# Seven-product first layers from block 11, exponentials read from PSUM, and a last tile stored in three pieces

## The chip, the cores and the metric

The kernel runs on one core of one Trainium2 chip. The metric is device time in microseconds (us), the median of the runs shown. An execution is one launch that goes through attention, one feed-forward layer and one gated layer for 36 tiles of 128 tokens.

## The reference

What is computed, cut to its steps (B = 8, 8 heads, 576 tokens, heads of 64, model width 512):

```python
# 1. attention in chunks of 64 tokens
scores = q_c @ k_c.T / 8
attn = exp(scores - scores.max(-1)); attn /= attn.sum(-1) + 1e-9
x = attn @ v_c                                  # [B, 576, 512]
# 2. a feed-forward layer
xn = (x - mean(x)) / sqrt(var(x) + 1e-6) * g_ln
x = x + relu(xn @ w_ch1) @ w_ch2                # 512 -> 2048 -> 512
# 3. a gated layer
u, v = split(gelu(x @ w_in))                    # 512 -> 2 * 512
v_s = w_sg @ (norm(v) * g_ln2) + b_sg           # over the 576 tokens
out = x + (u * v_s) @ w_out
```

## The kernel before

Every number goes through the matrix engine as a pair of 16-bit halves, so that a product of two tiles takes three matmuls (high by high, high by low, low by high).

Work is cut into **units** of 128 tokens (t = 0 to 35, attention and norm) and **blocks** of two units (b = 0 to 17, the feed-forward layer); the gated layer follows for all of them in a second part. Blocks 0 to 2 multiply in the plain way. From block B0 = 3 the second layer (`ff2p`, line 1005) takes **seven products** where eight would be plain. The first layer has two forms. `ff1p` (line 854, blocks 3 to 11) is plain: 192 matmuls of 256 columns in a block, in eight steps j of 24. `ff1s` (line 923, from block BS = 12) takes seven products over the block's two units: 336 matmuls of 128 columns. For `ff1s` the first-layer weights are summed and split again beforehand: `sums_w1` makes the sums, `move_w1` puts a part of them in place during the last `ff1p` block, and `norm7` (for units from 2*BS) prepares the block's input.

The weights of the gated layer are prepared during blocks 3 to 8 (`prep`, `halve`, `pieces`): ACT scales a piece into a scratch tile (`Btmp`), ACT copies the high half, DVE subtracts it for the low half. There is one scratch tile, so a piece's scaling waits for the subtraction of the one before. `sums_w1` starts when all pieces are done and stored (`close_st`).

A unit from t = 10 on goes like this. SP loads q and k (`qkl`) and v. PE makes the scores in one half of a PSUM pair (`qk`, line 302). DVE takes the maximum (line 400) and subtracts it into `pml` (line 401), ACT takes the exponential in place (line 404). ACT and DVE split that into two halves, SP turns them by DMA (line 415), and PE multiplies with v (`pv_`, line 360). The matmuls of lines 302 and 360 work on 64 by 64 parts of the array, all others of this stretch on the whole 128 by 128. The scores of unit t+1 are part of the same entry as `pv_` of unit t:

```python
o("PE", 1260, lambda: (pv_(), qk_()), rd=pp() + [a_], wr=[kp, ks])
```

The order on each engine is set by a **planner** (class `Plan`): each entry has an engine, a cost in ns, what it reads and writes, a latency and a priority; the planner simulates the engines and emits, on each, the entry of the lowest priority number among those that are ready. Attention has the numbers 10*t, the matmuls of the two layers have 1000 and up in the order of writing, what follows them on ACT and DVE has about -100, and the weights' preparation 8000 to 9000, so that it fills gaps. On the chip each engine takes its instructions in that order and waits for what they need.

The last tile of the second part (`o_unit`, line 2050) is done in two halves of 256 columns: for each half a slot of the ring `xp` is loaded (line 2044), DVE adds (line 2055), SP stores (line 2058).

Of the kernel before, what the change touches and what calls it, by code (L numbers as in the profile page):

```python
# [51 lines left out]
BS = 12  # L52
# [96 lines left out]
def fused_kernel(ctx: ExitStack, tc, qkv, w1, w2, g1, w_in, w_out, wsgt, wsgs, g2, b_sg, out):  # L149
# [162 lines left out]
    def attention(t):  # L312
# [19 lines left out]
        pm = palloc("pm", 2, [P, 4, 2, 64], F32) if t < JOIN else palloc("pml", 1, [P, 4, 2, 64], F32)  # L332
# [58 lines left out]
        def sums():  # L391
# [9 lines left out]
        o("DVE", 600, lambda: nc.vector.tensor_tensor(  # L401
            out=pm.t.rearrange("p h a k -> p a h k"), in0=sv, in1=mx.t.to_broadcast([P, 2, 4, 64]), op=ALU.subtract
        ), rd=[ks, mx], wr=[pm])
        o("ACT", 520, lambda: nc.scalar.activation(out=pm.t, in_=pm.t, func=AF.Exp, scale=0.125), wr=[pm], **far)
# [62 lines left out]
    def norm7(t, x, o):  # L467
# [38 lines left out]
        xT = xT_t[b] = plan.buf("xTD", 2, lambda: dl["all"][:, 7680 + n * 3584:11264 + n * 3584].rearrange(  # L506
# [578 lines left out]
    def open_b():  # L1085
        close_pool("sums")
        bW["wBp"] = tc.tile_pool(name="wB", bufs=1)
        wB = bW["wBp"].__enter__()
        bW["win"] = late[:, 0:8192].rearrange("p (k x e) -> p k x e", k=4, x=2)
        bW["winT"] = late[:, 8192:16384].rearrange("p (k u x n e) -> p k u x n e", k=2, u=2, x=2, n=4)  # L1090
        for nm, sh in (("wout", [P, 4, 2, D]), ("wsg", [P, 5, 2, S])):
            bW[nm] = wB.tile(sh, F16, name=nm)
        bW["stp"] = tc.tile_pool(name="stB", bufs=1)
        bW["st"] = bW["stp"].__enter__()
        bW["top"].t = bW["st"].tile([P, 1024], F32, name="top")
        nc.vector.memset(bW["top"].t, 0.0)
# [7 lines left out]
    half = []  # L1104

    def prep(nm, srcs):
# [37 lines left out]
    def halve(nm, n, i, m, q, full, ck):  # L1144
# [3 lines left out]
        def fin():  # L1148
# [11 lines left out]
        tmp = plan.buf("Btmp", 1, lambda: bW["st"].tile([P, 1024], F32, tag="tmp", name="tmp", bufs=1))  # L1160
# [3 lines left out]
            out=tmp.t[:, 0:P], in_=row.partition_broadcast(P)[:, 0, :]  # L1164
        ), rd=[f"redd{i}"], wr=[tmp], prio=pr, lat=5000)
        op("DVE", 220, lambda: nc.vector.tensor_reduce(
            out=col(nm + "_e"), in_=tmp.t[:, 0:P], axis=AX.X, op=ALU.max
# [53 lines left out]
    def sums_w1(j):  # L1221

        pr = 8000 + j
        n = j % 2
# [135 lines left out]
    with tc.manual_schedule():  # L1360
# [79 lines left out]
        half.append(prep("wsg", [wv[k] for k in range(4)] + [wsgs]))  # L1440
        done = [f"winT{k}{uv}" for k in range(2) for uv in range(2)] + [f"win{k}" for k in range(4)] + [f"wout{k}" for k in range(2)] + [f"wsg{k}" for k in range(5)]
        op(None, 0, lambda: None, wr=[f"w1_{j}" for j in range(8)], prio=0)
        todo = []
        for b in range(B0, BS):
# [10 lines left out]
            if b == B0 + 4:  # L1455
                op(None, 0, close_st, rd=["wsg_s"] + done + [f"{k}D" for k in done], wr=["Braw", "Btmp", "topB", "w1s"] + done, prio=0)
                for j in range(8):
                    sums_w1(j)
                op(None, 0, lambda: None, wr=["wb0", "wb1", "wt0", "wt1", "xTD0", "xTD1", "xTD0l", "xTD1l"], prio=0)
# [572 lines left out]
        def o_unit(g, i, more=False):  # L2032
# [5 lines left out]
            parts = 2 if t == NG * GT - GT + 4 else 1  # L2038
            for q in range(parts):
                (key, ap), = take(1)  # L2040
                m = 512 // parts
                fc = slice(q * m, q * m + m)
                xr = o_ring(more)
                do("SP", 730, lambda xr=xr, fc=fc: nc.sync.dma_start(out=xr.t[:, fc], in_=x2d[t][:, fc]), [], [xr], lat=2200)
# [8 lines left out]
                for h in range(2):  # L2053
                    pe(1300 // parts, lambda h=h, mm=mm: mm(h), ["gt0", "gt1"] if i == 4 else [f"gp{i // 5}{2 * h + k}" for k in range(2)], [key])
                do("DVE", 730 // parts, lambda xr=xr, fc=fc, ap=ap, m=m: nc.vector.scalar_tensor_tensor(
                    out=xr.t[:, fc], in0=ap[:, 0:m], scalar=col(cn), in1=xr.t[:, fc], op0=ALU.mult, op1=ALU.add
                ), [key, cn], [xr], 1000)
                do("SP", 730, lambda xr=xr, fc=fc: nc.sync.dma_start(out=out[t][:, fc], in_=xr.t[:, fc]), [xr], [], lat=2200)
# [142 lines left out]
```

## Time and profile before

| | |
|---|---|
| runs | 1161.77, 1162.14, 1162.97 us, median 1162.14 |
| the profiled execution | 1161.08 us, its span 1159.3 us |
| PE (matmuls), busy | 1143.9 us, 99% of the span |
| PEld (weight loads), busy | 896.1 us, 77% |
| DVE, busy | 956.7 us, 83% |
| ACT, busy | 729.4 us, 63% |
| POOL, busy | 171.2 us, 15% |
| TensorE clock granted, mean | 0.992 |
| chain that ended last, by engine | PE 92%, DVE 3%, DMA 2% |

Busy time and share of the span are for one engine each, and engines work beside each other. The chain is followed back from the last instruction, at each step to what released it. A matmul's own duration (273 ns for 256 columns) is longer than the distance to the next, since matmuls overlap; what counts for the time is that distance, from start to start.

### The profile page before, as it was taken

Reading aid. Unit: us, or ns where it says so; the run is one execution under the profiler, and the core shown is the slowest. Engines: PE = TensorE matmul, PEld = TensorE weight load, DVE = VectorE, ACT = ScalarE, POOL = GpSimd, SP = SyncE. Lnnn points to the kernel's source line nnn. Section 1 sums busy time; section 2 is a strip of 40 time slices with the busy share of each in tenths; the row PEclk is TensorE's granted clock in tenths of the full one; section 3 lists DMA queues with packets and bytes.
Section 4 is the critical chain, followed back from the end, with each engine's and each line's share of the span. In section 5 each row is a group of like instructions: output and inputs, shape, how many; then the busy total and the mean of one; then the engine's idle time right before and its main releaser. Section 6 shows DMA issues by size and latency. Waiting matters only on the chain.

```text
span 1159.3 us, 30389 instructions
## 1 busy us (share of the span) xinstructions
PE 1143.9 (99%) x12866; PEld 896.1 (77%) x12866; DVE 956.7 (83%) x1757; ACT 729.4 (63%) x1231; POOL 171.2 (15%) x285
## 2 busy tenths in 40 slices
PE   7999999999999999999999999999999999999998
PEld 5788448888888888888999999998566558558554
DVE  6997796999888899999887887896888688788555
ACT  5787645668667776666566666565748647646621
POOL 2211010223313223201011001001202101101100
PEclk7999999999999999999999999999999999999999
DMA  8964016546444532414352431696355481392203
GB/s 286 285 237 133 19 29 219 170 129 140 124 122 122 155 93 65 102 47 92 102 88 57 107 70 34 156 272 180 74 112 162 91 181 56 109 178 78 91 1 109
DMA packets 182824, 141.36 MB, mean 122 GB/s; under 512 B 142624, under 2 KB 151712, under 8 KB 182688
## 3 DMA queue, kind: packets, MB, share of 16 engines
q1 hardware_dynamic: 182688, 139.43, 45.3%
q8 instruction: 100, 1.64, 0.6%
q14 instruction: 36, 0.29, 0.1%
HBM read 79.46 MB, written 25.59 MB: 91 GB/s over the span
## 4 chain that ended last, share of the span: by engine, by line
PE 92%; DVE 3%; DMA 2%; ACT 1%; issue 1%; SPq 0%; POOL 0%; DVEq 0%; ACTq 0%
PE acc L1005 23%; PE bank L854 16%; PE bank L923 9%; PE pb L1853 4%; PE acc L1853 4%; PE pair L759 4%; PE bank L738 4%; PE acc L1741 3%; PE pb L1741 3%; PE pb L1799 3%; PE acc L1799 3%; PE pb L2050 3%; PE acc L1989 2%; PE bank L759 2%; PE pair L302 2%; PE pb L1989 1%
## 5 line engine op out<-in xcount | busy, mean ns | idle before, releaser
L1005 PEld LDWEIGHTS <-arena 128*128 128x128 f16 x2016 | 194.0, 98 | 22.3
L854 PE MATMUL bank<-xTo,w1all 128*128 128x256 f16 x1728 | 201.1, 273 | 0.0
L854 PEld LDWEIGHTS <-w1all 128*128 128x128 f16 x1728 | 168.5, 98 | 20.1
L1005 PE MATMUL acc<-w,arena 128*128 128x256 f16 x1152 | 174.2, 273 | 0.0
L1005 PE MATMUL acc<-w2s,arena 128*128 128x256 f16 x864 | 142.2, 273 | 0.0
L881 ACT ACTIVATE arena<-arena 128x896 f16<-128x896 f32 x72 | 68.2, 947 | 40.5 <-PE acc L1005 24.9
L882 DVE TENSOR_TENSOR arena<-arena 128x896 f16<-128x896 f32 x72 | 80.6, 1120 | 8.1 <-ACT arena L881 7.4
L869 ACT ACTIVATE arena<-bank 128x512 f32<-128x512 f32 x72 | 42.5, 591 | 51.8 <-PE bank L854 48.5
L923 PE MATMUL bank<-dL,w1all 128*128 128x128 f16 x1152 | 73.3, 219 | 1.1 <-ACT arena L936 0.5
L1741 PEld LDWEIGHTS <-x2T 128*128 128x128 f16 x672 | 65.5, 98 | 9.9
L923 PEld LDWEIGHTS <-w1all 128*128 128x128 f16 x1152 | 68.3, 98 | 2.6 <-issue 1.5
L1799 PEld LDWEIGHTS <-w1all 128*128 128x128 f16 x336 | 32.9, 98 | 38.4 <-issue 0.7
L738 PEld LDWEIGHTS <-w1all 128*128 128x128 f16 x576 | 54.8, 98 | 9.4 <-issue 1.6
L923 PE MATMUL bank<-dL,late 128*128 128x128 f16 x864 | 60.0, 219 | 0.3
L923 PEld LDWEIGHTS <-late 128*128 128x128 f16 x864 | 53.4, 98 | 2.0 <-issue 0.6
L1853 PEld LDWEIGHTS <-vh 128*128 128x128 f16 x288 | 28.5, 99 | 33.5
L1005 PEld LDWEIGHTS <-dL 128*128 128x128 f16 x504 | 47.1, 98 | 5.2 <-DVE dL L979 0.5
L1871 ACT ACTIVATE w2s<-uT 128x512 bf16<-128x512 f32 x30 | 18.8, 627 | 49.2 <-DVE uT L1867 43.8
L1853 PE MATMUL pb<-late,vh 128*128 128x512 f16 x150 | 46.7, 380 | 0.0
L738 PE MATMUL bank<-xTo,w1all 128*128 128x256 f16 x384 | 44.9, 273 | 0.9 <-DMA xTo<-hl 0.7
L1005 PE MATMUL acc<-w,dL 128*128 128x256 f16 x288 | 44.2, 273 | 0.2 <-DVE dL L979 0.2
L1853 PE MATMUL acc<-late,vh 128*128 128x512 f16 x138 | 42.6, 380 | 0.0
(390 smaller groups left out, 2672.6 us busy)
## 6 DMA issues: line engine op xcount, KB each, us to landing
straw<-in_w SPq DMA_DIRECT2D x16, 1023.8 KB, 6.3
qkl<-in_qkv SPq DMA_DIRECT2D x26, 512.0 KB, 3.8
x2d<-x SPq DMA_DIRECT2D x36, 256.0 KB, 2.0
vl<-in_qkv SPq DMA_DIRECT2D x26, 256.0 KB, 3.2
xz<-x2d SPq DMA_DIRECT2D x22, 256.0 KB, 3.4
xs<-x2d SPq DMA_DIRECT2D x21, 256.0 KB, 3.2
qk<-in_qkv SPq DMA_DIRECT2D x10, 512.0 KB, 5.1
wD<-late SPq DMA_DIRECT2D x8, 512.0 KB, 2.9
```

The source lines that it names most:

```text
L738: nc.tensor.matmul(acc, lhsT=w[j][:, k, fc], rhs=xT.t[:, x, k], start=(n == 0), stop=(n == 11))
L759: nc.tensor.matmul(acc[i], lhsT=h[x].t[:, c], rhs=w2t[j][:, f % 2, y], start=(f == 0 and n == 0), stop=(f == NF - 1 and n == 2),)
L854: nc.tensor.matmul(acc[:, y * 256:y * 256 + 256], lhsT=w[j][:, k, fc], rhs=xT.t[:, x, k], start=(n == 0), stop=(n == 11),)
L869: op("ACT", 500, lambda: nc.scalar.activation(out=o.t[:, 0:4].rearrange("p n t -> p (n t)"), in_=acc, func=AF.Relu, scale=0.5), rd=[kb] + ...
L881: op("ACT", 860, lambda: nc.scalar.activation(out=h.t[:, 0], in_=o.t[:, 1:8], func=AF.Copy), rd=[o] + ar, wr=[h], prio=-100)
L882: op("DVE", 1010, lambda: nc.vector.tensor_tensor(out=h.t[:, 1], in0=o.t[:, 1:8], in1=h.t[:, 0], op=ALU.subtract), rd=[o, h], wr=[h.key + ...
L923: nc.tensor.matmul(ap, lhsT=left(p, j, w, k), rhs=xT.t[:, x, SEVEN[p] * 2 + k], start=(first and n == 0), stop=(k == 1 and w == 1), skip_g ...
L1005: nc.tensor.matmul(acc, lhsT=h.at(x, n), rhs=r(y), start=(first and j == 0 and m == 0), stop=(j == 7 and m == 2), skip_group_check=True,)
L1741: nc.tensor.matmul(ap[:, q * 256:q * 256 + 256], lhsT=xT[:, x, a, k, c], rhs=right(b, 1, k, w), start=(first and n == 0), stop=(k == 1 and ...
L1799: nc.tensor.matmul(ap, lhsT=right(b, 0, k, w)[:, m * 128:m * 128 + 128], rhs=xT[:, x, a, k], start=(first and n == 0), stop=(k == 1 and w ...
L1853: nc.tensor.matmul(ap, lhsT=v[:, fc], rhs=w[:, 0:512], start=(n == 0), stop=end)
L1989: nc.tensor.matmul(bk[1][:, q * 256:q * 256 + 256], lhsT=gs[e][x][h][:, c:c + 128], rhs=r, start=(first and n == 0), stop=(k == 1 and x == ...
```

## The change

- **Seven-product first layers in seven blocks.** BS goes from 12 to 11: block 11 takes `ff1s` in place of `ff1p`, units 22 and 23 take `norm7`, `move_w1` runs during block 10. The scratch places of `sums_w1` and of the `xTD` buffers are laid out anew for it.
- **Weights' splits through three buffers.** `Btmp` becomes three scratch tiles (`rt`, cut in three, two of which are also the place of the raw load).
- **Exponentials per head from PSUM.** In units 10 to 21 the subtraction on DVE and the exponential over 512 columns go. POOL makes the maximum times -0.125, and ACT takes eight exponentials of 64 columns from PSUM with it as bias. `pml` gets two buffers.
- **`pv_` and `qk_` are two entries of the planner**, for all units from 10 on.
- **Last tile in pieces** of 256, 128 and 128 columns, with one load for all.

```diff
-BS = 12
+BS = 11
@@ attention
-        pm = ... palloc("pml", 1, [P, 4, 2, 64], F32)
+        pm = ... palloc("pml", 2, [P, 4, 2, 64], F32)
...
+        if 10 <= t < 22:
+            def less():
+                nc.gpsimd.tensor_scalar(out=mx.t, in0=mx.t, scalar1=-0.125, scalar2=0.0, op0=ALU.mult, op1=ALU.add)
+            def exps(a, hs):
+                for h in hs:
+                    nc.scalar.activation(
+                        out=pm.t[:, h, a], in_=s2[:, a, h * 64:h * 64 + 64], func=AF.Exp, scale=0.125, bias=mx.t[:, a, h]
+                    )
+            o("POOL", 300, less, wr=[mx], two=2)
+            for a_, hs in [(a_, range(h_, h_ + 4 // 4)) for a_ in range(2) for h_ in range(0, 4, 4 // 4)]:
+                o("ACT", 190, lambda a_=a_, hs=hs: exps(a_, hs), rd=[ks, mx], wr=[pm], **far)
+        else:
+...
...
-            o("PE", 1260, lambda: (pv_(), qk_()), rd=pp() + [a_], wr=[kp, ks])
+            o("PE", 330, pv_, rd=pp(), wr=[kp])
+            o("PE", 450, qk_, rd=[a_], wr=[ks])
@@ prep, halve, pieces
+    def rtmp(k):
+        c = (2048, 0, 1024)[k]
+        return plan.buf(f"Btmp{'abc'[k]}", 1, lambda: bW["rt"][:, c:c + 1024])
...
-            tmp = plan.buf("Btmp", 1, lambda: bW["st"].tile([P, 1024], F32, tag="tmp", name="tmp", bufs=1))
+            nt3[0] += 1
+            tmp = rtmp(nt3[0] % 3)
@@ sums_w1
-        n = j % 2
+        n = j % 2 if j < 6 else (NB - BS) % 2
@@ o_unit
-            parts = 2 if t == NG * GT - GT + 4 else 1
-            for q in range(parts):
+            xr = o_ring(more)
+            do("SP", 730, lambda: nc.sync.dma_start(out=xr.t, in_=x2d[t]), [], [xr], lat=2200)
+            for c, m in ((0, 256), (256, 128), (384, 128)) if t == NG * GT - GT + 4 else ((0, 512),):
                 (key, ap), = take(1)
-                m = 512 // parts
-                fc = slice(q * m, q * m + m)
-                xr = o_ring(more)
-                do("SP", 730, lambda xr=xr, fc=fc: nc.sync.dma_start(out=xr.t[:, fc], in_=x2d[t][:, fc]), [], [xr], lat=2200)
+                fc = slice(c, c + m)
```

The planner is run anew, so every engine's order moves from block 3 on. Three places:

**PE, the end of unit 20 in the kernel before** (`ptt` and `vq` are the two operands of `pv_`, `qkl` holds q and k of the next unit, `pair` is the PSUM pair; line 1005 is the second layer):

```order
L360 LDWEIGHTS ptt
L360 MATMUL pair_67<-vq,ptt 64x64
L302 MATMUL pair_67<-qkl 64x64 x16
L1005 LDWEIGHTS arena
L1005 MATMUL acc_2383<-w2s,arena 128x256
L1005 LDWEIGHTS arena
L1005 MATMUL acc_2383<-w2s,arena 128x256
```

**PE, the scores of the same next unit in the changed kernel** (line 870 is `ff1p`, 1021 the second layer):

```order
L870 LDWEIGHTS w1all
L870 MATMUL bank_69<-xTo,w1all 128x256
L302 MATMUL pair_67<-qkl 64x64 x16
L1021 LDWEIGHTS arena
L1021 MATMUL acc_2383<-w_5_176,arena 128x256
L1021 LDWEIGHTS arena
L1021 MATMUL acc_2383<-w_5_176,arena 128x256
```

**PE, a `pv_` in the changed kernel**, the next one behind those scores:

```order
L360 LDWEIGHTS ptt
L360 MATMUL pair_67<-vq,ptt 64x64
L360 LDWEIGHTS ptt
L360 MATMUL pair_67<-vq,ptt 64x64
L1021 LDWEIGHTS arena
L1021 MATMUL acc_2384<-w_1_172,arena 128x256
L1021 LDWEIGHTS arena
```

Before, 25 of the 26 score groups stand right behind a `pv_`; now one does, and the other 25 stand between whole-array matmuls, as one did before.

**ACT in block 5, from the first-layer result of its third step on**, before (line 869 is that result's ReLU, 881 its high half, 1199 and 1202 a weight piece's scaling and high half, 779 a maximum):

```order
L869 ACTIVATE arena<-bank_68 128x512
L1202 ACTIVATE late<-tmp 128x1024
L779 ACTIVATE u,x2mx<-x 128x512
L869 ACTIVATE arena<-bank_69 128x512
L881 ACTIVATE arena<-arena 128x896
L1199 ACTIVATE tmp<-late,c_win_s 128x1024
L1202 ACTIVATE late<-tmp 128x1024
L881 ACTIVATE arena<-arena 128x896
```

and changed, from the same ReLU (now lines 885 and 897; 1146 is a maximum of a weight, 408 an exponential of one head):

```order
L885 ACTIVATE arena<-bank_68 128x512
L408 ACTIVATE pml<-pair_67,mx 128x64
L1146 ACTIVATE rt,mxc<-wsg 128x576
L408 ACTIVATE pml<-pair_67,mx 128x64
L1146 ACTIVATE rt,mxc<-wsg 128x576
L408 ACTIVATE pml<-pair_67,mx 128x64
L1146 ACTIVATE rt,mxc<-wsg 128x576
L408 ACTIVATE pml<-pair_67,mx 128x64
L1146 ACTIVATE rt,mxc<-wsg 128x576
L408 ACTIVATE pml<-pair_67,mx 128x64
L795 ACTIVATE u,x2mx<-x 128x512
L897 ACTIVATE arena<-arena 128x896
L885 ACTIVATE arena<-bank_69 128x512
```

Exponentials of 64 columns now stand between the other work, and two scalings in a row become possible further on.

**SP, the last rows**, before (2044 loads a slot, 2058 stores):

```order
L2044 DMA xr_12738<-x2d_110 128x512
L2058 DMA out<-xr_12739 128x512
L2044 DMA xr_12739<-x2d_106 128x256
L2058 DMA out<-w2s 128x512 x3
L2058 DMA out<-g_12742 128x512
L2058 DMA out<-xr_12738 128x512
L2044 DMA w2s<-x2d_106 128x256
L2058 DMA out<-xr_12739 128x256
L2058 DMA out<-w2s 128x256
```

and changed (2065 loads, 2083 stores):

```order
L2065 DMA xr_12937<-x2d_110 128x512
L2083 DMA out<-xr_12938 128x512
L2065 DMA xr_12938<-x2d_106 128x512
L2083 DMA out<-w2s 128x512 x3
L2083 DMA out<-g_12941 128x512
L2083 DMA out<-xr_12937 128x512
L2083 DMA out<-xr_12938 128x256
L2083 DMA out<-xr_12938 128x128 x2
```

The second load of the last tile is gone from between the last stores, and the first loads all 512 columns.

## Rows read from the trace of the kernel before

**Rows 1.** The page's part 1: busy us, share, instructions of each engine

```profile
PE 1143.9 (99%) x12866; PEld 896.1 (77%) x12866; DVE 956.7 (83%) x1757; ACT 729.4 (63%) x1231; POOL 171.2 (15%) x285
```

**Rows 2.** Timeline of PE in block 11: start us, busy us, line, what, count

```profile
508.06 2.78 PE L854 MATMUL bank<-xTo,w1all 128*128 128x256 f16 x24
510.68 0.49 PE L1005 MATMUL acc<-w,arena 128*128 128x256 f16 x3
```

**Rows 3.** Timeline of PE in block 12, seven-product first layer

```profile
551.96 0.83 PE L923 MATMUL bank<-dL,late 128*128 128x128 f16 x12
552.63 0.49 PE L1005 MATMUL acc<-w2s,arena 128*128 128x256 f16 x3
```

**Rows 4.** Timeline of PE where pv_ and the next scores follow each other

```profile
411.52 0.49 PE L1005 MATMUL acc<-w2s,arena 128*128 128x256 f16 x3
411.94 0.58 PE L360 MATMUL pair<-vq,ptt 64*64 64x64 f16 x48
412.35 0.70 PE L302 MATMUL pair<-qkl 64*64 64x64 f32 x32
412.97 0.83 PE L1005 MATMUL acc<-w,arena 128*128 128x256 f16 x6
```

**Rows 5.** Timeline of PE where scores stand alone

```profile
187.42 0.82 PE L1005 MATMUL acc<-w,arena 128*128 128x256 f16 x6
188.16 0.69 PE L302 MATMUL pair<-qkl 64*64 64x64 f32 x32
188.79 0.50 PE L1005 MATMUL acc<-w2s,arena 128*128 128x256 f16 x3
```

**Rows 6.** Timeline of PE where a pv_ stands alone

```profile
704.04 0.83 PE L923 MATMUL bank<-dL,late 128*128 128x128 f16 x12
704.81 0.58 PE L360 MATMUL pair<-vq,ptt 64*64 64x64 f16 x48
705.32 0.50 PE L1005 MATMUL acc<-w,dL 128*128 128x256 f16 x3
```

**Rows 7.** Timeline of all engines at the end

```profile
1152.07 2.78 PE L2050 MATMUL pb<-late,w2s 128*128 128x256 f16 x24
...
1153.58 0.48 DVE L2055 SCALAR_TENSOR_TENSOR xr<-pb,c_c_m,xr 128x256 f32<-128x256 f32 x1 [0.56 <-PE pb L2050]
...
1155.97 0.48 DVE L2055 SCALAR_TENSOR_TENSOR w2s<-pb,c_c_m,w2s 128x256 f32<-128x256 f32 x1 [1.90 <-DMA w2s<-x2d]
1156.48 0.33 SPq L2058 DMA_DIRECT2D out<-w2s  x1
```

**Rows 8.** Whom PE waited for, 177 to 800 us: total, times, longest

```profile
PE bank L923 <- ACT arena L936: 0.5, 1, 0.5
PE bank L923 <- DVE dL L939: 0.4, 1, 0.4
PE bank L923 <- DVE arena L939: 0.3, 1, 0.3
PE acc L1005 <- DVE dL L979: 0.2, 1, 0.2
```

**Rows 9.** DVE from block 4 to block 7: window, its length, busy

```profile
239.60:344.50 104.90, 91.89 (x185) 1.00 0.53 130
```

**Rows 10.** ACT in the same window

```profile
239.60:344.50 104.90, 73.10 (x111) 1.00 0.53 130
```

**Rows 11.** Groups of DVE by shape: count, busy us, mean ns, idle before

```profile
L401 DVE TENSOR_TENSOR pml<-pair,mx 128x512 f32<-128x512 f32 x26 | 17.6, 678 | 0.0
...
L1205 DVE TENSOR_TENSOR late<-tmp,late 128x1024 f16<-128x1024 f32 x8 | 9.7, 1214 | 0.6 <-ACT late L1202 0.6
```

**Rows 12.** Groups of ACT by shape

```profile
L936 ACT ACTIVATE dL<-bank 128x256 f32<-128x256 f32 x48 | 18.3, 381 | 37.5 <-PE bank L923 33.8 <-DVE dL L979 2.6 <-DVE x L1030 0.9
...
L404 ACT ACTIVATE pml<-pml 128x512 f32<-128x512 f32 x26 | 16.1, 620 | 1.6 <-DVE pml L401 1.5
...
L1035 ACT ACTIVATE u<-acc,c_c2a 128x256 f32<-128x256 f32 x13 | 6.1, 472 | 1.1 <-PE acc L1005 0.7
```

More of the change, by code (lines that the diff above doesn't have):

```diff
@@ L331, in attention @@
         mx = palloc("mx", 2, [P, 2, 4, 1], F32)
-        pm = palloc("pm", 2, [P, 4, 2, 64], F32) if t < JOIN else palloc("pml", 1, [P, 4, 2, 64], F32)
+        pm = palloc("pm", 2, [P, 4, 2, 64], F32) if t < JOIN else palloc("pml", 2, [P, 4, 2, 64], F32)
         sm = palloc("sm", 2, [P, 4, 2, 1], F32)
@@ L400, in attention @@
         o("DVE", 600, lambda: nc.vector.tensor_reduce(out=mx.t, in_=sv, axis=AX.X, op=ALU.max), rd=[ks], wr=[mx])
[L401 to L404, printed above, removed]
+        if 10 <= t < 22:
[10 more added lines that the diff above has]
+        else:
+            o("DVE", 600, lambda: nc.vector.tensor_tensor(
+                out=pm.t.rearrange("p h a k -> p a h k"), in0=sv, in1=mx.t.to_broadcast([P, 2, 4, 64]), op=ALU.subtract
+            ), rd=[ks, mx], wr=[pm])
+            o("ACT", 520, lambda: nc.scalar.activation(out=pm.t, in_=pm.t, func=AF.Exp, scale=0.125), wr=[pm], **far)
         if t < BYDMA:
@@ L505, in norm7 @@
         plan.count["xTD"] = n - 1 if n else 1
-        xT = xT_t[b] = plan.buf("xTD", 2, lambda: dl["all"][:, 7680 + n * 3584:11264 + n * 3584].rearrange(
+        xT = xT_t[b] = plan.buf("xTD", 2, lambda: dl["all"][:, 7680 + n * 4096:11264 + n * 4096].rearrange(
             "p (x n t) -> p x n t", x=2, t=128
@@ L1095, in open_b @@
         bW["top"].t = bW["st"].tile([P, 1024], F32, name="top")
+        bW["rt"] = bW["st"].tile([P, 3072], F32, name="rt")
         nc.vector.memset(bW["top"].t, 0.0)
@@ L1163, in halve @@
         op("SP", 100, lambda: nc.sync.dma_start(
-            out=tmp.t[:, 0:P], in_=row.partition_broadcast(P)[:, 0, :]
+            out=bW["top"].t[:, 0:P], in_=row.partition_broadcast(P)[:, 0, :]
         ), rd=[f"redd{i}"], wr=[tmp], prio=pr, lat=5000)
         op("DVE", 220, lambda: nc.vector.tensor_reduce(
-            out=col(nm + "_e"), in_=tmp.t[:, 0:P], axis=AX.X, op=ALU.max
+            out=col(nm + "_e"), in_=bW["top"].t[:, 0:P], axis=AX.X, op=ALU.max
         ), rd=[tmp], wr=[nm + "_r"], prio=pr)
@@ L1455, in fused_kernel @@
             if b == B0 + 4:
-                op(None, 0, close_st, rd=["wsg_s"] + done + [f"{k}D" for k in done], wr=["Braw", "Btmp", "topB", "w1s"] + done, prio=0)
+                op(None, 0, close_st, rd=["wsg_s"] + done + [f"{k}D" for k in done], wr=["Btmpa", "Btmpb", "Btmpc", "topB", "w1s"] + done, prio=0)
                 for j in range(8):
                     sums_w1(j)
-                op(None, 0, lambda: None, wr=["wb0", "wb1", "wt0", "wt1", "xTD0", "xTD1", "xTD0l", "xTD1l"], prio=0)
+                for n in range(2):
+                    op(None, 0, lambda: None, wr=[f"wb{n}", f"wt{n}", f"xTD{n}", f"xTD{n}l"], prio=0)
             block(b + 2)
@@ L2053, in o_unit @@
                 for h in range(2):
-                    pe(1300 // parts, lambda h=h, mm=mm: mm(h), ["gt0", "gt1"] if i == 4 else [f"gp{i // 5}{2 * h + k}" for k in range(2)], [key])
-                do("DVE", 730 // parts, lambda xr=xr, fc=fc, ap=ap, m=m: nc.vector.scalar_tensor_tensor(
+                    pe(1300 * m // 512, lambda h=h, mm=mm: mm(h), ["gt0", "gt1"] if i == 4 else [f"gp{i // 5}{2 * h + k}" for k in range(2)], [key])
+                do("DVE", 130 + 600 * m // 512, lambda fc=fc, ap=ap, m=m: nc.vector.scalar_tensor_tensor(
                     out=xr.t[:, fc], in0=ap[:, 0:m], scalar=col(cn), in1=xr.t[:, fc], op0=ALU.mult, op1=ALU.add
-                ), [key, cn], [xr], 1000)
-                do("SP", 730, lambda xr=xr, fc=fc: nc.sync.dma_start(out=out[t][:, fc], in_=xr.t[:, fc]), [xr], [], lat=2200)
+                ), [key, cn, xr][:2 + (m < 512)], [xk], 1000)
+                do("SP", 730, lambda fc=fc: nc.sync.dma_start(out=out[t][:, fc], in_=xr.t[:, fc]), [xk], [], lat=2200)
         def wout_sums():
```

9 lines of the change are left out of this document (6 added, 3 removed).

## Prediction

> **What bounds the kernel now.** I read the page's first part, then the waits of PE, then PE's timeline at the places the change touches. PE is busy for 99% of the span, every other engine less [rows 1], and the chain of the table above is PE for 92% of it. The waits of PE from 177 to 800 us are four short ones, 1.4 us together, all in the blocks with seven-product first layers; none is in blocks 3 to 11 [rows 8]. So from block 3 on the time is the sum of the distances between matmul starts. An edit counts by what it adds to or takes from that sum, and by any new wait of PE. Only at the very end does something else come last: DVE's last addition starts when a load has landed, not when PE is done [rows 7].
>
> **Block 11 in seven products.** Plain: 24 matmuls of 256 columns take from 508.06 to 510.68, that is 0.109 us each [rows 2]; the block's 192 take 20.9 us. Seven products: 12 matmuls of 128 columns take from 551.96 to 552.63, 0.056 us each [rows 3]; 336 take 18.8 us. **Minus 2.2 us**, all of it on PE. The second layer stays as it is, and the first block of the new form with its start-up only moves one block earlier.
>
> The trace shows 0.056 us between 128-column matmuls although each has its own weight load [rows 3]. [...] The row decides: twelve in a row here take 0.67 us.
>
> **The last tile.** Before, PE's run of 24 matmuls ends at 1152.07 + 2.78 = 1154.85, but the last addition starts at 1155.97, held by the second load, takes 0.48 and the store is issued at 1156.48 [rows 7]. Now one load, early, feeds all pieces, and the order has no load between the last stores. PE's run keeps its length (12 x 0.109 + 24 x 0.056 = 2.65 against 24 x 0.109 = 2.62). The first half's addition begins at 1153.58, right when its twelve matmuls are through, so I let the last one follow PE at once: 1154.9, plus an addition of 128 columns (between 0.24, half of the 0.48 for 256, and 0.48; I take 0.36) gives 1155.3 for the store, against 1156.48. **Minus 1.2 us**; minus 0.9 if three stores close together land later, minus 1.5 if half the bytes land sooner.
>
> **`pv_` and `qk_` as two entries.** The words for the change don't mention it, and it is the largest term. No matmul is added. But these two work on 64 by 64 parts of the array, their neighbours on the whole, and each change between the two costs PE time. Together: the whole-array group before them would end at 411.52 + 3 x 0.109 = 411.85, the next whole-array matmul starts at 412.97: the pair takes 1.12 us of PE [rows 4]. Scores alone: 187.42 + 6 x 0.109 = 188.07 to 188.79, 0.72 us [rows 5]. A `pv_` alone: 704.04 + 0.67 = 704.71 to 705.32, 0.61 us [rows 6]. Apart they cost 0.72 + 0.61 - 1.12 = 0.21 us more. By the order, scores stand alone 25 times where they stood alone once: 24 x 0.2 = **plus 4.9 us** (4.8 to 5.0). Nothing hides it: PE has no waits there that it could fill [rows 8].
>
> [...]
>
> **Exponentials from PSUM.** In 12 units DVE loses a subtraction of 0.68 us [rows 11] and ACT an exponential of 0.62; ACT gets eight of 64 columns [rows 12]. No row shows one. An ACT pass from PSUM over 256 columns takes 0.38 us, with a scale per partition 0.47 [rows 12]; from 512 columns (0.62) to 256 (0.38) a column costs 0.93 ns, so 64 columns with a bias per partition come to 0.47 - 192 x 0.00093 = 0.29 us (0.12 if all of the 0.47 went by columns, 0.47 if none did). Eight take 2.4 us, 1.8 more than before. ACT is not the bound, so by itself this costs nothing. It counts where PE waits for it: the scores of the next unit now stand in PE's queue right behind these exponentials, whose PSUM they overwrite, and all of PE's matmuls are queued behind them. The planner reckons 8 x 0.19 = 1.5 us for the eight and keeps 1.0 us until the scores; the eight take 0.9 longer. So this cover is almost used up: between 0 and 0.4 us in each of 12 units.
>
> **Splits through three buffers.** The same work, earlier. Between the middle of block 4 and block 7 DVE is busy for 91.9 of 104.9 us [rows 9] and ACT for 73.1 [rows 10], so 13.0 and 31.8 are free. Counting the instructions between the same first-layer steps in both orders, each at its group's mean, DVE gets 14.3 us more there (the largest item four more weight pieces of 1.22, against five subtractions of 0.68 [rows 11]) and ACT some 30 with exponentials at 0.29. Both engines are full there. What covers it: a first-layer result is needed only two steps later, and no row of blocks 3 to 11 has PE wait for one [rows 8]. The summed weights for the first new block are done in DVE's order before step 6 of block 10, so block 11 doesn't wait for them.
>
> For the new waits of both kinds I take **plus 0.6 us**: from minus 0.8 (some of the 1.4 us of present waits fall away with the new order) to plus 5 (12 times 0.4).
>
> **Sum.** -2.2 - 1.2 + 4.9 + 0.6 = +2.1 us. The profiled execution, 1161.08 us, would be 1163.2; it lies 1.1 under the median, so the median 1162.14 becomes **1164.2**. A measurement of this kernel can tell about 0.2%, 2.3 us: faster is under 1159.8, slower over 1164.5.
>
> **The rivals.**
> - *PE waits for the exponentials and for two full engines.* Place: the scores behind the exponentials, units 10 to 21, and the second layer in blocks 4 to 7. It decides from an exponential of 0.31 us on, where eight are a full microsecond over the planner's figure. At 0.35 the eight take 2.8, 0.3 past the cover, 12 times: 3.6 us in place of 0.6, **1167.2**, slower. For it: both windows are full [rows 9, 10]. Against: PE itself runs later than the planner thinks by the very cost of the separate entries, which gives the others time. 17 in 100.
> - *The separate entries cost nothing*, since other waits would have stood in the same place: -2.2 - 1.2 + 0.6 = -2.8, **1159.3**, faster. Against it are three places that agree [rows 4 to 6] and a queue without waits. 5 in 100.
> - [...] 4 in 100.
> - *128-column matmuls go at the pace of their weight loads.* PEld is busy 896.1 us for 12866 loads [rows 1], 0.070 each: 336 would take 23.4, plus 2.5 where I have minus 2.2, **1168.9**, slower. [...] Against it stands the 0.67 for twelve [rows 3]. 1 in 100.
> - *The seven-product part doesn't pay*, since the new block brings waits like those of the six present ones, 1.4 us for six [rows 8], 0.2 each: too small to be told apart, in the 0.6.
>
> **How the numbers follow.** The forecast has 73 in 100; with 1161.8 to 1166 as its own spread around 1164.2, close under the line of 1164.5, I give 47 of them to within 0.2% and 26 to slower. With the rivals: faster 5, within 0.2% 51, slower 44. Leaving out the upper part of the first rival, the second and the fourth, the range is 1161.8 to 1167.0.
>
> **What would show it.** Right: the lone scores of the changed kernel take 0.72 us from whole-array matmul to whole-array matmul, the lone `pv_` 0.61; block 11 is some 2 us shorter apart from that; the last addition follows PE; PE's waits from 177 to 800 us stay under 3 us. Wrong: scores that wait for ACT in the waits of PE (first rival), or a pair apart that costs no more than 1.12 (second).

## The result, and the profile after

The changed kernel is slower: 1173.88 us median (1171.22 to 1174.9) against 1162.56, a ratio of 1.0103 with a 95% interval of 1.0087 to 1.0119. The prediction was 1164.2, with a range up to 1167.0. The sign of its sum was right, and three of its four terms; the fourth, the new waits, was far too small.

The profiled execution took 1171.22 us, its span 1169.4 (before: 1159.3). It lies 2.7 under the median of its kernel; what the three others spend more isn't known, since they have no trace. So the accounts below explain a rise of 10.1 us, that of the profiled executions, and not quite the 11.3 of the medians. The page's part 1 of the changed kernel, for [rows 1]:

```profile
PE 1146.0 (98%) x13022; PEld 894.5 (76%) x13022; DVE 955.3 (82%) x1746; ACT 744.1 (64%) x1326; POOL 172.3 (15%) x295
```

PE is busy hardly longer (2.1 us), while the span grew by 10.1: most of the rise is time in which PE stood idle. Whom PE waited for in the changed kernel, 177 to 805 us (total, times, longest), for [rows 8]:

```profile
PE pair L302 <- ACT pml L408: 4.2, 1, 4.2
PE pair L360 <- DMA ptt<-ph: 2.0, 1, 2.0
PE bank L939 <- ACT arena L952: 0.9, 2, 0.5
PE pair L360 <- DVE mx L400: 0.9, 1, 0.9
```

Two waits of block 5 are new and long: scores on an exponential (L408), `pv_` on the turned `ptt`. The chain of waits of the changed kernel in that stretch (start, us, what) tells where the first comes from:

```profile
270.31 7.62 DMA redd<-redc
...
278.05 0.33 SPq L1186
...
278.48 4.53 DMA x2d<-x
...
283.13 0.70 DVE x L457
...
283.85 0.32 ACT pml L408
...
284.22 1.13 PE pair L302 x32
285.35 2.67 PE bank L870 x12
```

Read it from the top. `redd<-redc` stores the 128 maxima of one weight, 4 bytes from each partition; line 1186 loads them back, all 128 to every partition. That load stands on SP's queue right behind the store, and SP stands at it until the store has landed, 7.6 us later. The stores of `x` to `x2d` are queued behind. DVE's write of a unit's attention into `x` (L457) needs the buffer that one of them empties and waits 7.8 us for it, the last of the eight exponentials of a unit waits 5.8 us for L457, and PE's next scores wait for that exponential. The wait of DVE, and what SP stood at its loads in all (the second time for 8.8 us, until 303.2; the `ptt` that PE waits for 2.0 us could be turned only behind that, at 303.70):

```profile
DVE x L457 <- DMA x2d<-x: 7.8, 1, 7.8
```

```profile
SPq L1186 <- DMA redd<-redc: 15.8, 2, 8.8
```

Then the clock: windows ahead of the long wait, behind it, and later (start and end, length, busy us with the number of instructions for PE, PEld, DVE, ACT and POOL, granted clock, DMA share, GB/s):

```profile
256.96:279.70 22.74, 22.74 (x321) 19.85 (x319) 16.79 (x37) 19.34 (x47) 9.72 (x12) 1.00 0.42 115
284.22:290.00 5.78, 5.78 (x55) 4.31 (x56) 5.71 (x13) 5.49 (x7) 1.64 (x4) 0.50 0.78 147
290.20:300.00 9.80, 9.80 (x135) 8.61 (x134) 9.73 (x18) 9.17 (x16) 5.74 (x6) 1.00 0.33 124
```

After PE had stood still for 4.2 us its granted clock was 0.50 for 5.8 us, and 1.00 again in the window from 290.20: by the account below that cost 2.3 us.

The order had shown the cause, in rows that I did not read. SP in block 5 in the kernel before:

```
L1162 DMA redd_73<-redc 128x1
L1163 DMA tmp<-redd_72 128x128
L330 DMA vl<-in_qkv 128x512
L1162 DMA redd_74<-redc 128x1
L278 DMA_TRANSPOSE xTo<-hl 128x8x128
L777 DMA x2d_83<-x 128x512
L777 DMA x2d_84<-x 128x512
```

and changed:

```
L1185 DMA redd_73<-redc 128x1
L1186 DMA top<-redd_73 128x128
L793 DMA x2d_83<-x 128x512
L793 DMA x2d_84<-x 128x512
L430 DMA_TRANSPOSE ptt<-ph 128x8x128
```

Before, the loads went into the one scratch tile `Btmp`, which the pieces kept in use, so each came long after its store (the load of `redd_73` started at 291.93, its store at 260.67). Now they go into `top`, which is free. These lines of the change do that; the excerpt of the diff ahead doesn't show them:

```diff
-        tmp = plan.buf("Btmp", 1, lambda: ...)
+        tmp = Buf("topB", None)
...
-            out=tmp.t[:, 0:P], in_=row.partition_broadcast(P)[:, 0, :]
+            out=bW["top"].t[:, 0:P], in_=row.partition_broadcast(P)[:, 0, :]
```

Nearly all of the difference between the two traces has its place. The **account** below goes by the starts of PE's matmuls in each profiled execution, from the first first-layer matmul of block 3 to the last one of the second layer. *Pace*: whole-array matmuls times 0.1087 us (256 columns) or 0.056 (128). *Modes*: 0.603 for each lone `pv_`, 0.721 for lone scores, 1.123 for both together. *Waits*: what distances between starts exceed that by 0.06 us or more. *Half clock*: matmuls at 0.214 where 0.109 is the pace (up to 0.2 are single distances in kernels whose granted clock was never down). The rest is 1.8 to 2.3 in all of them. *After* is from there to PE's last matmul. The kernels were measured in four groups, each beside the kernel before, which had medians of 1162.56, 1161.21, 1161.85 and 1160.90: compare by the ratio, which is taken within a group.

| kernel | pace | modes | waits | half clock | after | median | ratio to before, 95% |
|---|---|---|---|---|---|---|---|
| before | 574.8 | 29.4 | 2.6 | 0.0 | 367.7 | 1162.56 | |
| changed | 572.7 | 34.2 | 10.0 | 2.3 | 367.7 | 1173.88 | 1.0087 to 1.0119 |
| a_late | 572.7 | 34.2 | 6.1 | 0.1 | 368.0 | 1165.56 | 1.0021 to 1.0055 |
| a_pool | 572.7 | 34.2 | 2.9 | 0.1 | 367.7 | 1163.31 | 1.0000 to 1.0026 |
| b_top | 574.8 | 29.4 | 4.5 | 0.0 | 367.7 | 1164.38 | 1.0000 to 1.0039 |
| a_noexp | 572.7 | 34.4 | 13.7 | 3.4 | 367.7 | 1176.91 | 1.0095 to 1.0155 |
| b_exps | 574.8 | 29.4 | 22.8 | 2.1 | 373.7 | 1192.15 | 1.0265 to 1.0298 |
| b_split | 574.8 | 34.4 | 11.1 | 0.0 | 367.9 | 1177.76 | 1.0094 to 1.0161 |
| a_merge | 572.7 | 29.4 | 18.5 | 1.8 | 375.8 | 1183.23 | 1.0143 to 1.0213 |
| a_pool_m780 | 572.7 | 29.4 | 27.6 | 7.5 | 372.7 | 1192.34 | 1.0229 to 1.0283 |
| b_bs_tail | 572.7 | 29.4 | 14.0 | 2.2 | 368.3 | 1172.07 | 1.0060 to 1.0098 |
| b_tail | 574.8 | 29.4 | 3.0 | 0.2 | 369.0 | 1160.12 | 0.9982 to 1.0006 |
| a_pool_merge_noexp | 572.7 | 29.4 | 16.6 | 2.7 | 368.6 | 1175.51 | 1.0119 to 1.0150 |

For the changed kernel: -2.1 (pace), +4.8 (modes), +7.4 (waits), +2.3 (half clock), +0.3 (rest); the stretch ahead of block 3 was 1.3 shorter in this execution (it differs by as much between kernels whose order is the same there), and the end behind PE's last matmul 1.4 shorter. That is +10.0 of the 10.1 by which the span grew.

### The profile page after: what moved, and what is told of

Same layout as the page of the kernel before. It is cut to its first block, busy times and chain, and to the rows that moved or that the text cites. A ratio compares the mean times of both kernels' runs of the same rounds, so it can differ in the third digit from the quotient of the medians.

```text
span 1169.4 us, 30807 instructions
## 1 busy us (share of the span) xinstructions
PE 1146.0 (98%) x13022; PEld 894.5 (76%) x13022; DVE 955.3 (82%) x1746; ACT 744.1 (64%) x1326; POOL 172.3 (15%) x295
## 4 chain that ended last, share of the span: by engine, by line
PE 87%; DVE 6%; DMA 3%; ACT 2%; issue 1%; POOL 0%; SPq 0%; ACTq 0%; DVEq 0%; POOLq 0%
PE acc L1021 21%; PE bank L870 12%; PE bank L939 11%; PE pb L1879 4%; PE acc L1879 4%; PE pair L775 4%; PE bank L754 3%; PE acc L1767 3%; PE pb L1767 3%; PE pb L2075 3%; PE pb L1825 3%; PE acc L1825 3%; PE acc L2015 2%; PE bank L775 2%; PE pb L2015 1%; PE pair L302 1%
## 5 line engine op out<-in xcount | busy, mean ns | idle before, releaser
L1021 PEld LDWEIGHTS <-arena 128*128 128x128 f16 x1932 | 184.8, 98 | 23.7 <-ACT arena L994 0.8
L870 PE MATMUL bank<-xTo,w1all 128*128 128x256 f16 x1536 | 180.7, 274 | 0.0
L870 PEld LDWEIGHTS <-w1all 128*128 128x128 f16 x1536 | 150.0, 98 | 18.5
L897 ACT ACTIVATE arena<-arena 128x896 f16<-128x896 f32 x64 | 60.9, 952 | 40.8 <-PE acc L1021 24.7
L939 PE MATMUL bank<-dL,w1all 128*128 128x128 f16 x1344 | 85.2, 219 | 0.9 <-ACT arena L952 0.9
L898 DVE TENSOR_TENSOR arena<-arena 128x896 f16<-128x896 f32 x64 | 70.0, 1094 | 9.6 <-ACT arena L897 9.4
L939 PE MATMUL bank<-dL,late 128*128 128x128 f16 x1008 | 70.0, 219 | 0.0
L939 PEld LDWEIGHTS <-late 128*128 128x128 f16 x1008 | 62.1, 98 | 1.6
L1021 PEld LDWEIGHTS <-dL 128*128 128x128 f16 x588 | 55.1, 98 | 5.7
L1021 PE MATMUL acc<-w,dL 128*128 128x256 f16 x336 | 51.6, 273 | 0.0
L754 PE MATMUL bank<-xTo,w1all 128*128 128x256 f16 x384 | 44.9, 273 | 1.9 <-DMA xTo<-hl 1.7
L952 ACT ACTIVATE dL<-bank 128x256 f32<-128x256 f32 x56 | 21.3, 380 | 38.5 <-PE bank L939 35.1
```

The costliest lines, as they stand in the source:

```text
L754: nc.tensor.matmul(acc, lhsT=w[j][:, k, fc], rhs=xT.t[:, x, k], start=(n == 0), stop=(n == 11))
L870: nc.tensor.matmul(acc[:, y * 256:y * 256 + 256], lhsT=w[j][:, k, fc], rhs=xT.t[:, x, k], start=(n == 0), stop=(n == 11),)
L897: op("ACT", 860, lambda: nc.scalar.activation(out=h.t[:, 0], in_=o.t[:, 1:8], func=AF.Copy), rd=[o] + ar, wr=[h], prio=-100)
L898: op("DVE", 1010, lambda: nc.vector.tensor_tensor(out=h.t[:, 1], in0=o.t[:, 1:8], in1=h.t[:, 0], op=ALU.subtract), rd=[o, h], wr=[h.key + ...
L939: nc.tensor.matmul(ap, lhsT=left(p, j, w, k), rhs=xT.t[:, x, SEVEN[p] * 2 + k], start=(first and n == 0), stop=(k == 1 and w == 1), skip_g ...
L1021: nc.tensor.matmul(acc, lhsT=h.at(x, n), rhs=r(y), start=(first and j == 0 and m == 0), stop=(j == 7 and m == 2), skip_group_check=True,)
```

## The experiments

Kernels a_... are the changed one with something undone, b_... are the one before with one part of the change.

### The load behind its store

The planner's ready time of an entry adds the latency of what it reads only where the two are on different engines; from SP to SP it adds 130 ns. So it thinks that a load may follow the store that it reads at once. The first experiment puts an entry without an engine between them, so that a latency counts, and makes it 9 us:

```diff
-        op("SP", 60, ... out=redd[i], in_=redc[:, i:i + 1] ..., wr=[f"redd{i}"], prio=pr, lat=5000)
+        op("SP", 60, ... out=redd[i], in_=redc[:, i:i + 1] ..., wr=[f"redd{i}"], prio=pr, lat=9000)
+        op(None, 0, lambda: None, rd=[f"redd{i}"], wr=[f"reddw{i}"], prio=pr, lat=0)
...
-        ), rd=[f"redd{i}"], wr=[tmp], prio=pr, lat=5000)
+        ), rd=[f"reddw{i}"], wr=[tmp], prio=pr, lat=5000)
```

> The changed kernel, with the three loads of a weight's maxima placed some 9 us behind the store that they read, in place of right behind it in SP's order; up to the first of them every order stays. Theory A (SP's queue): in the changed kernel SP stands at that load for the 7 to 9 us that the store takes to land, and the stores of x and the turning of ptt behind it start late. Then PE's waits of 4.2 us (scores on an exponential) and 2.0 us (pv_ on ptt) go, with the 2.2 us of half clock behind the first: 1173.9 - 8.9 = 1165.0, 0.3% above before. Theory B (eight exponentials of 0.32 us are too slow for the scores behind them): nothing of this changes, 1173 to 1175.

Measured: 1165.56, where 1165.0 was expected by theory A (its 8.9 us are 0.5 more than the three items that it names). The kernel before had 1161.21 beside it, so 4.4 us are left of the 11.3: some 7 are gone, 6.1 of them by the account (3.9 of waits, 2.2 of half clock). The wait on `ptt` and the half clock are gone; 2.6 us of waits for exponentials stay. Why they stay is seen at the stores. The DMA view of this kernel from 269 to 282 us (busy tenths and GB/s in 40 slices of 0.325 us, then issues with their median us from issue to landing), and the longest wait of DVE:

```profile
DMA  0069998000497000039900000000000000000000
GB/s 0 0 115 216 207 195 126 0 0 0 139 391 271 6 0 0 0 126 384 296 0 0 0 0 0 0 0 0 0 0 0 0 0 0 0 0 0 0 0 0
...
x2d<-x SPq DMA_DIRECT2D x2, 256.0 KB, 7.4
...
redd<-redc SPq DMA_DIRECT2D x1, 0.5 KB, 8.7
```

```profile
DVE x L457 <- DMA x2d<-x: 5.3, 1, 5.3
```

The two bursts near 390 GB/s are the stores of `x`, issued 1.8 and 4.1 us behind the small store. Their bytes are through by 275.5, and the DMA engines stand idle from then on; yet both count as landed only at 280, after the small one at 278.5. So a load at which SP waits is one part of the harm; the other is that this store of 128 pieces of 4 bytes took 8.7 us to land, and that the two stores behind it counted as landed only after it.

The next one issues the small stores from POOL:

```diff
+        op("POOL", 60, lambda: nc.gpsimd.dma_start(out=redd[i], in_=redc[:, i:i + 1]), ..., lat=9000)
```

> As the run with the loads 9 us later, but the stores of a weight's maxima (128 rows of 4 bytes) are issued by POOL, on its own queue. With the later load, a store of x issued at 271.62 right behind such a store still landed only at 280.05, where others take 2.0 us. Theory D (on one queue a store is reported landed only after the one ahead of it): now the stores of x land in 2 to 3 us, DVE's wait of 5.3 us for one goes, and with it PE's 2.6 us of waits for exponentials: 1163.0 on the scale where the later load gave 1165.6. Rival E (the small pieces hold the DMA engines themselves): the stores of x still take 6 to 9 us, 1165.6.

Measured: 1163.31; its waits of PE are down to those of before:

```profile
PE bank L939 <- ACT arena L952: 0.9, 2, 0.5
PE acc L1021 <- ACT arena L994: 0.5, 1, 0.5
```

The time is that of theory D, but not its reason. POOL issued the small store at 273.62, and it landed at 281.84. Of the two stores of `x` the one issued at 273.02 landed in 2.1 us, the one at 275.32 in 9.7, at 285.02 (DMA view of this kernel, 272.5 to 273.5 and 275.2 to 276):

```profile
x2d<-x SPq DMA_DIRECT2D x1, 256.0 KB, 2.1
```

```profile
x2d<-x SPq DMA_DIRECT2D x1, 256.0 KB, 9.7
```

So another queue did not free what was issued behind: 9.7 us for the store issued 1.7 us after the small one. The store that DVE waited for merely came ahead of the small one now. Theory D (one queue) falls. In both kernels the stores issued behind the small one landed after it (at 280 against 278.5 in a_late, at 285.02 against 281.84 in a_pool). Why they do isn't shown, nor what the 3.2 us between 281.84 and 285.02 are, and no trace here tells which of the DMA engines carried the small pieces.

Rival E (the small pieces hold the DMA engines) is contradicted by the idle slices of a_late, but not done with: in a_noexp, the next section's kernel, a load of 512 KB (`qkl`) was issued between the small store (228.62) and the two stores of `x` (232.80 and 235.11). Single packets of that load (4 KB) took up to 7.9 us, and the packets of the stores (2 KB) are recorded only from 242.0 to 243.9, after the small store had landed at 239.5. From 234.3 to 241.5 us the DMA engines moved less than 100 GB/s (DMA view, 228 to 246 us, slices of 0.45 us):

```profile
DMA  5799473290909900969557699622115999700000
GB/s 182 208 268 139 95 81 40 46 264 8 64 18 100 9 0 18 91 73 36 18 46 27 36 27 46 18 9 9 9 18 209 387 391 414 269 23 0 0 0 0
...
qkl<-in_qkv SPq DMA_DIRECT2D x1, 512.0 KB, 11.3
x2d<-x SPq DMA_DIRECT2D x2, 256.0 KB, 10.1
...
redd<-redc SPq DMA_DIRECT2D x1, 0.5 KB, 10.9
```

So what is shown is that transfers behind such a store came late in these three kernels. In a_late the bytes were through by 275.5 and only the landing was late, at 280; in a_noexp the bytes were late too, at 242.0 to 243.9. Why that is, and why 512 bytes took 8.7 us, is not settled by any run here.

The reverse, the kernel before with the target of these loads as the only edit (the planner's order follows it):

```diff
-        tmp = plan.buf("Btmp", 1, lambda: ...)
+        tmp = Buf("topB", None)
```

> The kernel before, with one thing changed: the maxima of a weight are read back into the scratch tile that is free (top), in place of the one that the pieces use. By the order the three loads then stand one or two rows behind their stores on SP, as in the changed kernel. Theory A: SP stands there for the 7 to 9 us that such a store takes to land, stores of x and turnings of ptt behind it start late, DVE waits some 5 to 8 us for a store of x, and part of that reaches PE: 1165 to 1171. Rival: the two steps of cover between the layers hide it, and only the changed kernel with its other orders was hurt: 1162.

Measured: 1164.38, 2.5 over the kernel before beside it, with a lower bound of the interval at no change. By this time alone the effect isn't shown. The trace has the mechanism, smaller: SP stood at these loads for 11.4 us in two waits, and PE for a `ptt` that was turned behind them:

```profile
PE pair L360 <- DMA ptt<-ph: 1.8, 1, 1.8
```

DVE did not wait for a store of `x` here, so where the queue's delay strikes depends on the rest of the order.

### The exponentials

```diff
-        if 10 <= t < 22:
+        if False:
```

> The changed kernel with the subtraction on DVE and one exponential of 512 columns again in units 10 to 21; all else as changed. Theory A: the loads of a weight's maxima still stand one or two rows behind their stores on SP, so some of the 8.9 us stays, if the delayed addition into x reaches PE by another way: 1166 to 1174. Theory B: the waits of PE come from the exponentials alone: 1165, and no wait of PE over 1 us. A third theory C: both are needed, since the exponentials read the PSUM pair that the delayed addition reads, and so wait for it: 1165 too, but with DVE still seen waiting for the store of x.

Measured: 1176.91, over all the expectations. The delayed write of `x` (the "addition" of the expectations, L457) reaches PE without any exponential. Of PE and of DVE in this kernel:

```profile
PE acc L1021 <- DVE arena L898: 3.6, 1, 3.6
```

```profile
DVE x L457 <- DMA x2d<-x: 7.1, 1, 7.1
```

Right behind that write (243.76) DVE has the low halves of the first layer (L898, 244.37), and PE's second layer waits for one. In this stretch SP did not stand at a load: it issued the two stores of `x` at 232.80 and 235.11, and they landed 10.9 and 9.2 us later, as shown above. So theories B and C fall; the exponentials were one road from DVE's wait to PE, not its cause. The other waits of this kernel (13.7 us in all) come with its new order.

The exponentials alone, in the kernel before (the diff of the change, with `pml` in two buffers):

> The kernel before with the exponentials from PSUM in units 10 to 21 alone, pv_ and the next scores still one entry. The eight take 8 x 0.318 = 2.5 us on ACT where one took 0.62, and DVE is spared 12 x 0.68. If they hold up the scores by themselves (first rival of the prediction): waits of PE for ACT in most of the 12 units, 1164 to 1168. If only a late addition into x holds them, since both read one PSUM pair: at most two such waits, and the time is set by how the planner's new order falls out: 1161 to 1166.

Measured: 1192.15, but not by what either theory says. In this trace nobody waits for an exponential of 64 columns. The long wait of PE comes after the last of the 12 units:

```profile
PE bank L869 <- DMA xTo<-hl: 11.5, 1, 11.5
```

The input of block 10 is late: POOL takes four additions of a block's output (4.47 us from 470.77) ahead of the `hl` that SP then turns, though ACT was done with its half of `hl` at 470.94. The planner ordered it so. That is 4.3 of the 11.5 us; the rest of the lateness lies ahead of it and isn't followed here.

In the changed kernel the exponential that PE waited for had itself waited for DVE's L457 (ACT waited for it 6.9 us in three waits, the longest 5.8), although both only read there: the scores lie in columns 0 to 255 and the result of `pv_` in columns 256 to 511 of the same two halves of the PSUM pair. The planner doesn't know of that wait: it books the two as `pair1` and `pairv`. Why the program waits there isn't shown by any run.

### One entry or two

> The kernel before, with pv_ and the next scores as two entries, and nothing else changed. By the rows 24 x 0.2 us: 1162.2 + 4.8 = 1167.0, with 0.72 us for scores alone and 0.60 for pv_ alone. If the separate entries cost nothing: 1162.2. If a change of mode costs half: 1164.6.

> The changed kernel with pv_ and the next scores as one entry again. If the 0.2 us for each separated pair is a real price of PE time, 24 of them go: 1173.9 - 4.8 = 1169.1 with the waits of block 5 as they are (theory A: the loads still stand right behind their stores). If the separate entries cost nothing, 1174. If the waits of block 5 come from the scores' own place behind the exponentials, and not from SP, they go as well: 1160.

> As the run before, with pv_ and the next scores as one entry again, at the planner's cost of the two (780 ns), not the 1260 of the kernel before. The 0.2 us of each separated pair go: -4.8, so 1158 to 1160. If one entry brings waits of its own, as it did with 1260 (18.5 us of waits in place of 10.0): 1165 to 1175.

The edit of b_split is that of the change; a_merge undoes it, and a_pool_m780 does with 780 in place of 1260:

```diff
-            o("PE", 330, pv_, rd=pp(), wr=[kp])
-            o("PE", 450, qk_, rd=[a_], wr=[ks])
+            o("PE", 1260, lambda: (pv_(), qk_()), rd=pp() + [a_], wr=[kp, ks])
```

The price of a separated pair is what the rows said, in every kernel: lone scores 0.721, lone `pv_` 0.602 or 0.603, together 1.121 to 1.123, so 4.8 us of modes for 24 pairs, 5.0 for the 25 of b_split. The changed kernel's timeline of PE, lone scores and a lone `pv_`:

```profile
262.49 2.78 PE L870 MATMUL bank<-xTo,w1all 128*128 128x256 f16 x24
265.20 0.69 PE L302 MATMUL pair<-qkl 64*64 64x64 f32 x32
265.83 0.50 PE L1021 MATMUL acc<-w,arena 128*128 128x256 f16 x3
...
268.13 1.47 PE L870 MATMUL bank<-xTo,w1all 128*128 128x256 f16 x12
269.54 0.58 PE L360 MATMUL pair<-vq,ptt 64*64 64x64 f16 x48
270.04 1.49 PE L870 MATMUL bank<-xTo,w1all 128*128 128x256 f16 x12
```

And yet the times are 1177.76, 1183.23 and 1192.34, where 1167.0, 1169.1 and 1158 to 1160 were the main expectations. In each, waits decide: 11.1 us in b_split against 2.6 before; 18.5 in a_merge against 10.0 in the changed kernel; 27.6 and 7.5 of half clock in a_pool_m780 against 2.9 and 0.1 in a_pool. In the last two the second part (*after*) is longer too, by 8.1 and 5.0. The longest of a_merge (one entry, 1260) are the second layer's inputs and the turned input of a seven-product block:

```profile
PE acc L1020 <- DVE arena L994: 5.6, 3, 3.0
PE bank L938 <- DMA dL<-xTo: 2.6, 1, 2.6
```

With one entry the scores of unit t+1 can't stand ahead of `pv_` of unit t; in the changed kernel they do (two groups of scores, at 187 and 197 us, come before the first `pv_` at 207). That would give the exponentials' side more time, and explain why two entries were chosen together with the rest. It is argued from the order; no run isolates it.

### Seven products and the last tile

```diff
-BS = 12
+BS = 11
...
-            parts = 2 if t == NG * GT - GT + 4 else 1
+            xr = o_ring(more)
+            for c, m in ((0, 256), (256, 128), (384, 128)) if t == NG * GT - GT + 4 else ((0, 512),):
```

> The kernel before with two parts of the change alone: block 11 in seven products, and the last tile in pieces. By the accounts of the two traces: -2.1 and -1.4, 1158.0 where before has 1161.5. Rival: the planner's new order and the new block bring waits, 0.6 us each as in the blocks of this kind: 1159 to 1162.

Measured: 1172.07, with one wait of 9.6 us at the first seven-product block:

```profile
PE bank L923 <- ACT dL L936: 10.7, 3, 9.6
```

PE waits for ACT to read the first bank of block 11 (L936). In ACT's order that read stands behind the high half of a summed weight (L1248), for which ACT stood 3.9 us until DVE's sums (L1243) were there:

```profile
519.46 1.54 DVE L1243 TENSOR_TENSOR dL<-dL 128x256 f32<-128x256 f32 x4
```

```profile
521.03 0.84 ACT L1248 ACTIVATE late<-dL 128x768 f16<-128x768 f32 x1 [3.91 <-DVE dL L1243]
...
522.09 0.36 ACT L936 ACTIVATE dL<-bank 128x256 f32<-128x256 f32 x1
```

L1243 and L1248 are part of `sums_w1`: the summed weights of the first layer are still being made when block 11 has started on seven products. In the last kernel of this section, which has three scratch buffers, there is no wait over 1.1 us at block 11. So the part with three buffers seems to pay for the seven products: without the earlier splits they start a block too early. That is argued from these two kernels, which differ in more than the buffers; no run has the three buffers alone.

The last tile alone (the lower part of that diff):

> The kernel before with the last tile in pieces alone; the first part's order stays as it is. In the changed kernel's trace the span ends 3.3 us after the start of PE's last matmul, in the trace of before 4.7: so -1.4, 1160.4 on a scale where before has 1161.8. If the end is set by something else here: 1161.8. No waits are added in either case.

Measured: 1160.12 where the kernel before had 1160.90 beside it, a ratio of 0.9994 that this measurement can't tell from 1. The profiled execution has a wait of 1.2 us in the second part that the kernel before hasn't, so *after* is 1.3 longer. The end itself does what was expected: the last addition starts 0.2 us behind the start of PE's last matmul (1158.3), where it was 1.4 us before (1154.6, against the 1155.97 of [rows 7]).

```profile
1157.18 0.48 DVE L2054 SCALAR_TENSOR_TENSOR xr<-pb,c_c_m,xr 128x256 f32<-128x256 f32 x1 [0.56 <-PE pb L2049]
1157.85 0.35 DVE L2054 SCALAR_TENSOR_TENSOR xr<-pb,c_c_m,xr 128x128 f32<-128x128 f32 x1 [0.18 <-PE pb L2049]
1158.52 0.35 DVE L2054 SCALAR_TENSOR_TENSOR xr<-pb,c_c_m,xr 128x128 f32<-128x128 f32 x1 [0.32 <-PE pb L2049]
```

All but two parts: the edits of a_pool, a_noexp and a_merge in one kernel.

> All of the change but the two parts that lengthen PE's or ACT's work: pv_ and the next scores one entry (1260) and one exponential of 512 columns again, and the stores of a weight's maxima on POOL's queue. Three scratch buffers, block 11 in seven products and the last tile in pieces stay. By the accounts -2.1 and -1.4: 1158.3 on a scale where before has 1161.8, if the weights' sums are ready for block 11 as in the changed kernel and no wait is added. If the planner's new order brings waits as in the other runs with one entry (18.5 and 27.6 us where before has 2.6): 1170 to 1185.

Measured: 1175.51. Block 11 is fed in time, but the new order has some twenty waits, 16.6 us, the longest 2.6 at a turned input. No kernel here is clearly faster than the one before.

## Why the prediction was wrong, point by point

- **Block 11 in seven products**, -2.2: 2.1 by the account. Right. That it needs the weights' sums in time was read off the changed order, and held.
- **The last tile**, -1.2: 1.4. Right.
- **Two entries**, +4.9: 4.8, at 0.20 for each pair. Right, and the rival in which the entries cost nothing is out. The chances hold 4 in 100 for about half of this price; no run shows such a term, and the times of lone and joint entries showed 0.20 us for each pair in its place.
- **The new waits**, +0.6 with a range of -0.8 to +5: **this step failed**. They were +7.4, and 2.3 of half clock behind them, together 9.7. With this in place of 0.6 the sum is +11.2. The profiled execution rose by 10.1, with a stretch ahead of block 3 that happened to be 1.3 shorter; that 11.2 lies so near to the 11.3 of the median is in part luck.

The failed step has two faults. The first is an omission. I took the splits through three buffers for "the same work, earlier" and costed DVE and ACT; the edit also moves the read-back of the maxima from the busy scratch tile to `top`. A DMA was moved past a queue, and I named neither it nor the stores and turnings of SP behind it. Three things were there to see: in the order, the load right behind its store; in the planner, no latency from SP to SP; in the trace of before, what such a store takes to land (8.7 and 8.8 us). With one such stand of SP and no cover, the upper end of the term would have lain at 8 us and more.

The second, less sure, is the size of the spread. In the seven kernels whose whole order from block 3 on was worked out anew by an edit to units, entries or blocks, the waits were 11 to 28 us, where the kernel before has 2.6; where only the loads' place or target differed (a_late, a_pool, b_top) they were 3 to 6. So a new order can bring 10 us and more, and a range of 3 us above the sum did not allow for it. It need not bring them: the order of the changed kernel is new as well, and without the queue's fault (a_pool) it has 2.9, as predicted. That this order has so few because its parts were chosen together is a guess; no run tests it.

The first rival was right on where PE would wait (scores behind exponentials) and on the exponential: 0.318 us, where it should decide from 0.31. So its sign, scores that wait for ACT, came true. But it was wrong on why, and that the sign came true is luck: no such wait came in 11 of the 12 units, nor in any of the 12 of b_exps. The groups of ACT, changed kernel, for [rows 12]:

```profile
L408 ACT ACTIVATE pml<-pair,mx 128x64 f32<-128x64 f32 x96 | 26.1, 318 | 8.6 <-DVE x L457 6.9 <-PE pair L360 0.8 <-POOL mx L404 0.7
```

The rival of 128-column matmuls at the pace of their weight loads is out too: in block 11 of the changed kernel 36 take 2.01 us from start to start, 0.056 each.

```profile
522.31 2.17 PE L939 MATMUL bank<-dL,w1all 128*128 128x128 f16 x36
524.32 0.83 PE L939 MATMUL bank<-dL,late 128*128 128x128 f16 x12
524.99 0.49 PE L1021 MATMUL acc<-w,arena 128*128 128x256 f16 x3
```

In the kernel without the queue's fault (a_pool) the sum as predicted (+2.1) holds: -2.1, -1.3 at the end, +4.8 and +0.4 of waits and half clock make +1.8, and its span is 1161.0 against 1159.3.

## What to carry to other kernels

Where a buffer's change frees a transfer to be issued earlier, look at what stands behind it on its issuing queue: here a load that waited for a store's landing held SP, and what was queued behind, for 7.0 and 8.8 us (changed kernel), and such a store, 128 pieces of 4 bytes, took 8.7 and 8.8 us to land in the trace of before. Where a planner sets the order, read the whole difference of the order around every DMA, and check whether its latencies count between entries of one engine. And give each new order a spread of its own: the price of an edit by its rows was right to 0.2 us, while the waits that came with a new order were between 0.3 us (a_pool) and 25.

## What the runs showed of the hardware that was not expected

- A store of 512 bytes in 128 pieces took 6.7 (b_exps) to 12.5 us (b_bs_tail) to land, where one of 256 KB takes 2.0 in the median (before, changed). Stores issued 1.7 to 4.1 us behind it landed only after it, on another queue too (a_pool). In a_late the DMA engines were idle meanwhile (275.5 to 280); in a_noexp the bytes themselves moved late (242.0 to 243.9, issued at 232.80 and 235.11).
- PE's granted clock was down at 0.50 for 5.8 us behind a standstill of 4.2 us, and at 0.50 in b_bs_tail behind one of 9.6; after the wait of 2.0 us in the changed kernel it stayed at 1.00. The length of one wait does not settle it: in a_pool_m780 the clock fell 1.0 us behind a wait of 2.0 us too (703.89). The windows behind the waits of 9.6 us (b_bs_tail) and 2.0 us (changed kernel):

```profile
522.50:528.50 6.00, 4.83 (x43) 4.50 (x43) 1.75 (x5) 1.45 (x4) 0.00 (x0) 0.50 0.80 147
```

```profile
305.20:312.00 6.80, 4.82 (x88) 4.11 (x86) 5.40 (x16) 4.51 (x6) 0.00 (x0) 1.00 1.09 283
```

- An exponential of 64 columns from PSUM with a bias per partition takes 0.318 us on ACT (the prediction estimated 0.29): eight of them 2.5 us, four times one of 512 columns (0.62 us, [rows 12]).
